# Loading the weights of groups 2 to 4 from SyncE instead of GpSimd in a fused attention and FFN backward kernel

## The chip, the cores and the metric

The kernel runs on one core of one Trainium2 chip. The metric is the device time of one execution in microseconds; the kernel before takes 282.91 us in the median of three runs (282.87 to 283.6). PE is the matrix engine, DVE the vector engine, ACT the scalar engine, POOL is GpSimd and SP is SyncE, which in this kernel does nothing but start DMA transfers.

## The reference, cut to what matters

One decode step with batch 4, model width 512, 32 query heads, 8 key/value heads of width 128 and a window of 1024 cached positions, next to a gated FFN of width 1792. The kernel returns the output and the gradients of all inputs:

```
xn  = layernorm(x)                                   # x: 4 x 1 x 512
q   = (xn @ wq) in 32 heads;  k, v = last 1024 of 4096 cached rows, each head used by 4 queries
o   = softmax(q k^T / sqrt(128)) v
out = x + o @ wo + (gelu(xn @ w_gate) * (xn @ w_up)) @ w_down
return out, d/d(x, k_cache, v_cache, wq, wo, w_gate, w_up, w_down) of <out, grad_out>
```

The gradients of the two caches have the shape of the caches, 4 x 8 x 4096 x 128 each in bf16. Three quarters of them (the rows outside the window) are zero and have to be written all the same. So there is far more to move than to compute: the profile counts 81.01 MB written to memory and 30.68 MB read.

## The kernel before, in words

The FFN part comes first; its three weight matrices lie in a pool that is closed when it is done. Then the attention part runs over four groups t = 0..3 of two key/value heads each (`for t in range(NT)`, line 725). A group needs its keys and values (`kb`, `vb`: two tiles of 1 MiB each, lines 127 to 135) and its slices of the output and query weights (`wo_sb`, `wq_sb`: 1 MiB each, lines 120 to 125). In a group:

- `pre(t)` (line 285) transposes `wo_sb` on PE (L279), multiplies with `wq_sb` (L303), and makes the query rows and the output-gradient rows. It is called for group t+1 in the middle of group t.
- `kv_steps(t, 0, 0)` and `kv_steps(t, 1, 1)` (line 335) transpose the keys and then the values block by block and form the scores and their gradient.
- `softmax`, `softmax_d`, `odq`, `odT` make probabilities and their gradients and the two products with values and keys.
- `fin(t)` (line 537) reads `wo_sb` (L256) and `wq_sb` (L279, `wqT_ps`) a last time; after that the two buffers are free.
- `dvdk` (line 475) makes the cache gradients in eight pieces per tile: a matmul (L484), a copy from PSUM into `stg_dv` or `stg_dk` by ACT or DVE (L97, L98), and after the eighth piece one 1 MiB store. The staging pool has three buffers. `dw(t)` (line 498) makes the weight gradients through `osb_o` and `osb_q`, of 512 KiB a store, from a pool of four.

The pieces of `dvdk` and `dw` stand in a list `bg`, and `tick(n)` takes n of them between the steps of the next group. All engines run their instructions in the order in which the program gives them; there is no scheduler (`manual_schedule`).

The order of transfers matters here. Every store, every zero fill (`zero()`, line 161: a store of 1.5 MiB from a tile of zeros, 32 in all) and every load but two kinds goes out on SP, in program order. SP waits in front of a transfer until its data or its buffer is ready, and everything behind waits too. The framework also gives the transfers started by SP and ACT eight completion semaphores in turn, so one of them is started only when the one eight places before it has landed. The transfers that POOL starts have semaphores of their own and a DMA queue of their own (q0 in the profile; SP's is q1). ACT starts three: `wg_sb` at the beginning and two small outputs at the end.

The line that decides the engine is the default of this argument; group 0 is loaded with `load_w(0, nc.sync)` on line 151, the others by POOL:

```
120    def load_w(t, eng=nc.gpsimd):
121        pool = w_pool[t % 2]
122        wo_t[t] = pool.tile([P, HG, D], BF16, name="wo_sb", tag="wo")
123        eng.dma_start(out=wo_t[t][:], in_=wo_v[t])
124        wq_t[t] = pool.tile([P, ND, CW], BF16, name="wq_sb", tag="wq")
125        eng.dma_start(out=wq_t[t][:], in_=wq_v[t])
```

In memory a row of a `wo` slice is 1 KB long (512 bf16 values) and a row of a `wq` slice 2 KB (1024 values).

Of the kernel before, what the change touches and what calls it, by code (L numbers as in the profile page):

```python
# [18 lines left out]
def kernel(  # L19
# [28 lines left out]
    nc = tc.nc  # L48
# [71 lines left out]
    def load_w(t, eng=nc.gpsimd):  # L120
        pool = w_pool[t % 2]
        wo_t[t] = pool.tile([P, HG, D], BF16, name="wo_sb", tag="wo")
        eng.dma_start(out=wo_t[t][:], in_=wo_v[t])
        wq_t[t] = pool.tile([P, ND, CW], BF16, name="wq_sb", tag="wq")
        eng.dma_start(out=wq_t[t][:], in_=wq_v[t])

    def load_kv(t, k):
        if t >= NT:
            return
        d_, src, nm = ((k_t, A_k_cache, "kb"), (v_t, A_v_cache, "vb"))[k]  # L130
        for g in range(GP):
            tl = kv_pool[t % 2].tile([P, JB, Dh], BF16, name=nm, tag=nm)
            nc.sync.dma_start(out=tl[:].rearrange("p j d -> p (j d)"),
                              in_=src[:, t * GP + g, K0:Sk, :].rearrange("b (m j) d -> m b (j d)", j=JB))
            d_[(t, g)] = tl
# [25 lines left out]
    def zero(n=1):  # L161
        for _ in range(min(n, len(zlist))):
            og, b, g = zlist.popleft()
            store(nc.sync, og[b, g:g + ZR, 0:K0, :].rearrange("g (m j) d -> m g (j d)", m=P // ZR), ztile[:], "zeros")
# [103 lines left out]
    def link(n=1):  # L268
        for _ in range(min(n, len(chain))):
            chain.popleft()()  # L270
# [64 lines left out]
    def kv_steps(t, k, links):  # L335

        zt = (qm_all, dom_all)[k][t % 2]
        blks = (k_t, v_t)[k]
        ps = ps_a.tile([P, WQ], FP32, name="S_ps", tag=("S", "dP")[k])
        st[t][("S", "dP")[k]] = ps[:]  # L340

        def mm(g, q, T_sb):
            c0 = SL - 1 - (g * NQ + q)
            for b in range(B):
                nc.tensor.matmul(ps[b * RB:(b + 1) * RB, :], lhsT=zt[:, b * GP + g, c0:c0 + RB],  # L345
                                 rhs=T_sb[:].rearrange("p (x b) -> p b x", b=B)[:, b, :], start=(g == 0 and q == 0),
                                 stop=(g == GP - 1 and q == NQ - 1), tile_position=(0, b * RB))

        last = None
        for g in range(GP):  # L350
            for q in range(NQ):
                T_ps = transposes([blks[(t, g)][:, q * JQ + j, :] for j in range(JQ)], "T")
                T_sb = tsb.tile([P, JQ * P], BF16, name="T_sb", tag="T")
                evac(T_sb[:], T_ps[:].rearrange("p j x -> p (j x)"), 1024, half=True)
                tick(1)
                link(links)
                if last:
                    mm(*last)
                last = (g, q, T_sb)
                tick(1)  # L360
                link(links)
        mm(*last)
# [57 lines left out]
    def softmax_d(t):  # L420
        s = st[t]

        def a():
            s["Gt"] = attw.tile([P, WQ], FP32, name="Gt", tag="Gt")
            s["gs"] = attw.tile([P, 1], FP32, name="gs", tag="gs")
            nc.vector.tensor_tensor_reduce(out=s["Gt"][:], in0=s["E"][:], in1=s["dP"], scale=1.0, scalar=0.0,
                                           op0=ALU.mult, op1=ALU.add, accum_out=s["gs"][:])

        def b():
            gs_ps = ps_w.tile([P, 1], FP32, name="gs_ps", tag="w")  # L430
            nc.tensor.matmul(gs_ps[:], lhsT=rsum_f, rhs=s["gs"][:], start=True, stop=True)
            cc = attw.tile([P, 1], FP32, name="cc", tag="cc")
            nc.vector.tensor_tensor(out=cc[:], in0=gs_ps[:], in1=s["rr"][:], op=ALU.mult)
            nc.vector.scalar_tensor_tensor(out=s["Gt"][:], in0=s["dP"], scalar=cc[:, 0:1], in1=s["E"][:],
                                           op0=ALU.subtract, op1=ALU.mult)
            s["dS"] = spread(s["Gt"], s["rr"], "dS_s")

        def c():
            s["dST"] = transposed(s["dS"], "dST")

        idle = lambda: None
        chain.extend([a, idle, b, idle, c])
# [24 lines left out]
    def odT(t, k):  # L467
        rows = st[t][("o", "dq")[k]]
        T_ps = transposes([rows[:, g, :] for g in range(GP)], "odT")
        rT = attw.tile([P, GP, B, rep], BF16, name="od_T", tag=f"od_T{k}")  # L470
        for g in range(GP):
            nc.vector.tensor_copy(out=rT[:, g].rearrange("p b r -> p (b r)"), in_=T_ps[:, g, g * 32:g * 32 + B * rep])
        st[t][("oT", "dqT")[k]] = rT
# [243 lines left out]
    with tc.tile_pool(name="kv_b", bufs=GP, reuse_waits="tile") as kv_b, \  # L717
            tc.tile_pool(name="w_b", bufs=1, reuse_waits="tile") as w_b, \
            tc.tile_pool(name="stage", bufs=3, reuse_waits="tile") as stage:
        kv_pool[1], w_pool[1] = kv_b, w_b  # L720
        zero()
        pre(0)
        load_w(1)
        load_kv(1, 0)
        for t in range(NT):
            kv_steps(t, 0, 0)
            if t == 0:
                zero()
                load_kv(1, 1)
                zero()  # L730
            softmax(t)
            kv_steps(t, 1, 1)
            if t == NT - 1:
                zero(4)
            link(len(chain))
            softmax_d(t)
            link()
            odq(t, 0)
            load_kv(t + 2, 1)
            if t + 1 < NT:  # L740
                pre(t + 1)
            link(len(chain))
            odT(t, 0)
            odq(t, 1)
            load_kv(t + 2, 0)
            tick(2)
            odT(t, 1)
            fin(t)
            if t + 2 < NT:
                load_w(t + 2)  # L750
            (k0, k1), (o0, o1, q0, q1) = dvdk(t, 1), dw(t)
            for p in (k0, o0, k1, o1, q0, q1):
                bg.extend(p)
        tick(len(bg))
        zero(len(zlist))

        fin_ps = []
        for o in range(2):
            f_ps = ps_w.tile([B, ND, P], FP32, name="f_ps", tag="w")
            for c in range(ND):  # L760
                nc.tensor.transpose(f_ps[:, c, :], acc[:, o, c, :], ident_f[:])
            fin_ps.append(f_ps)
        acc_o = fin_ps[0][:].rearrange("b c p -> b (c p)")
        acc_d = attw.tile([B, P, ND], FP32, name="acc_d", tag="P_s")
        nc.vector.tensor_copy(out=acc_d[:].rearrange("b p c -> b c p"), in_=fin_ps[1][:])
        acc_d = acc_d[:].rearrange("b p c -> b (p c)")
        out_b = attw.tile([B, D], BF16, name="out_b", tag="pT")
        nc.vector.tensor_tensor(out=out_b[:], in0=acc_o, in1=x4[:], op=ALU.add)
        nc.scalar.dma_start(out=out_0.rearrange("b s d -> (b s) d"), in_=out_b[:])

        s1 = attw.tile([B, 1], FP32, name="s1", tag="m")
        nc.vector.reduce_sum(out=s1[:], in_=acc_d, axis=AX.X)
        pr = attw.tile([B, D], FP32, name="pr", tag="dS_s")
        s2 = attw.tile([B, 1], FP32, name="s2", tag="es")
        nc.vector.tensor_tensor_reduce(out=pr[:], in0=acc_d, in1=xn_f[:], scale=1.0, scalar=0.0,
                                       op0=ALU.mult, op1=ALU.add, accum_out=s2[:])
        nm1 = attw.tile([B, 1], FP32, name="nm1", tag="rr")
        nc.vector.tensor_scalar(out=nm1[:], in0=s1[:], scalar1=-1.0 / D, scalar2=None, op0=ALU.mult)
        nm2 = attw.tile([B, 1], FP32, name="nm2", tag="gs")
        nc.vector.tensor_scalar(out=nm2[:], in0=s2[:], scalar1=-1.0 / D, scalar2=None, op0=ALU.mult)  # L780
        nc.vector.scalar_tensor_tensor(out=pr[:], in0=xn_f[:], scalar=nm2[:, 0:1], in1=acc_d,
                                       op0=ALU.mult, op1=ALU.add)
        nc.vector.tensor_scalar(out=pr[:], in0=pr[:], scalar1=nm1[:, 0:1], scalar2=rstd[:, 0:1],
                                op0=ALU.add, op1=ALU.mult)
        dx_b = attw.tile([B, D], BF16, name="dx_b", tag="E_f")
        nc.vector.tensor_tensor(out=dx_b[:], in0=pr[:], in1=dy4[:], op=ALU.add)
        nc.scalar.dma_start(out=out_1.rearrange("b s d -> (b s) d"), in_=dx_b[:])
# [30 lines left out]
```

## Time and profile before

| what | value |
|---|---|
| median of three runs | 282.91 us |
| profiled execution, its own time | 283.0 us |
| its span from first to last instruction | 281.0 us |
| PE, DVE, ACT, POOL busy | 72%, 58%, 42%, 14% of the span |
| mean granted PE clock | 0.901 |
| bytes moved, mean rate | 112.12 MB, 399 GB/s |
| POOL's loads of the weights | 6 transfers of 1024 KB, 14.7 us (`wo_sb`) and 19.1 us (`wq_sb`) from issue to landing in the median |

The profiled execution takes 2.0 us more than its span, which lie outside the recorded instructions. Busy shares are means over a kernel with different stages. The row "DMA" of the page cuts the span into 40 slices of 7.0 us and shows the busy share of the 16 DMA engines in tenths (9 is 90% or more); "GB/s" is what they moved. A landing time runs from the issue of a transfer to its completion and includes the time that it stands behind others in its queue.

### The profile page before, as it was taken

The numbers are of one execution on the slowest core, as the hardware profiler recorded it, in microseconds if no ns is written. First come the engines' busy times: TensorE is split into PE (matmuls) and PEld (weight loads), VectorE is DVE, ScalarE is ACT, GpSimd is POOL, SyncE is SP. The second block draws the span as 40 slices with busy tenths as digits, with TensorE's granted clock in tenths as the row PEclk, the third lists the DMA queues.
The fourth block names the chain that finished last, engine by engine and source line by source line (L and its number), as shares of the span: only waits on it lengthen the run. The fifth ranks groups of instructions, "written<-read, shape, count | busy, mean of one in ns | idle before, by whom it ended". The sixth has DMA issues, their size and how long they took to land.

```text
span 281.0 us, 6867 instructions
## 1 busy us (share of the span) xinstructions
PE 203.1 (72%) x2972; PEld 138.8 (49%) x2972; DVE 164.1 (58%) x313; ACT 117.8 (42%) x219; POOL 40.1 (14%) x40
## 2 busy tenths in 40 slices
PE   0276699959789889998999299898999599390000
PEld 0265476735456665566775156677556484140000
DVE  7946646645776655577666067767677728386000
ACT  2030386635035418764448056443866038370000
POOL 8600000007002150002250000223000400000000
PEclk9999589986999999999999969999999979977555
DMA  7999999999999999999999999999999999999990
GB/s 264 393 375 431 431 426 417 425 419 424 369 395 424 422 420 420 426 415 422 419 417 411 412 424 423 431 383 398 385 368 415 387 432 410 425 429 422 398 422 30
DMA packets 19565, 112.12 MB, mean 399 GB/s; under 512 B 1664, under 2 KB 4496, under 8 KB 11088
## 3 DMA queue, kind: packets, MB, share of 16 engines
q1 hardware_dynamic: 17744, 103.56, 89.6%
q0 software_dynamic: 1632, 6.29, 5.6%
q10 hardware_dynamic: 160, 1.84, 1.9%
q8 instruction: 23, 0.38, 0.5%
q14 instruction: 6, 0.05, 0.0%
HBM read 30.68 MB, written 81.01 MB: 397 GB/s over the span
## 4 chain that ended last, share of the span: by engine, by line
PE 47%; DMA 22%; DVE 16%; ACT 4%; issue 2%; SPq 0%; DVEq 0%; ACTq 0%
DMA out_dram<-stg_dv 13%; PE T_ps L279 8%; PE kv_ps L484 7%; DMA wd_sb<-in_B_w_down_dram 6%; PE S_ps L345 5%; PE od_ps L450 5%; DMA out_dram<-osb_g 4%; DVE T_sb L98 3%; DVE dS_s L367 2%; PE wdT_ps L279 2%; PE dwq_ps L520 2%; PE acc_ps L256 2%; PE dwd_ps L660 2%; DVE P_s L367 2%; PE wgT_ps L279 2%
## 5 line engine op out<-in xcount | busy, mean ns | idle before, releaser
L98 DVE COPY T_sb<-T_ps 128x1024 bf16<-128x1024 bf16 x64 | 44.1, 688 | 26.7 <-PE T_ps L279 26.5
L97 ACT CAST stg_dk<-kv_ps 128x512 bf16<-128x512 f32 x52 | 29.2, 588 | 31.2 <-PE kv_ps L484 12.4
L97 ACT CAST stg_dv<-kv_ps 128x512 bf16<-128x512 f32 x51 | 28.1, 588 | 24.9 <-PE kv_ps L484 24.3
L484 PE MATMUL kv_ps<-qmr,dS_s 128*128 128x512 bf16 x64 | 23.9, 414 | 11.3 <-ACT stg_dk L97 10.6
L463 POOL TENSOR_TENSOR o_s<-od_r,msk_r 128x512 bf16<-128x512 bf16 x8 | 9.1, 1157 | 110.2 <-DVE od_r L455 80.9
L484 PE MATMUL kv_ps<-domr,P_s 128*128 128x512 bf16 x64 | 21.3, 382 | 0.0
L279 PE MATMUL T_ps<-ident,vb 128*128 128x128 bf16 x256 | 20.3, 225 | 0.4 <-DVE T_sb L98 0.4
L279 PE MATMUL T_ps<-ident,kb 128*128 128x128 bf16 x256 | 20.4, 225 | 0.0
L279 PEld LDWEIGHTS <-kb 128*128 128x128 bf16 x256 | 17.5, 101 | 4.5 <-issue 1.3
L279 PEld LDWEIGHTS <-vb 128*128 128x128 bf16 x256 | 17.2, 101 | 5.0 <-issue 3.2
L97 ACT CAST osb_q<-dwq_ps 128x512 bf16<-128x512 f32 x25 | 14.6, 587 | 8.3 <-PE dwq_ps L520 7.4
L329 POOL TENSOR_TENSOR domr<-r,msk 128x1024 bf16<-128x1024 bf16 x4 | 7.6, 1892 | 71.2 <-DVE r L326 65.1
L97 ACT CAST osb_g<-dwg_ps 128x512 bf16<-128x512 f32 (+1 forms) x25 | 12.3, 544 | 12.3 <-PE dwg_ps L673 6.3
L97 ACT CAST osb_o<-dwo_ps 128x512 bf16<-128x512 f32 x24 | 13.9, 586 | 4.5 <-PE dwo_ps L505 2.9
L98 DVE CAST stg_dk<-kv_ps 128x512 bf16<-128x512 f32 x12 | 8.0, 688 | 12.0 <-DMA out_dram<-stg_dv 11.2
L98 DVE COPY wgT<-wgT_ps 128x1024 bf16<-128x1024 bf16 x14 | 9.6, 686 | 6.8 <-PE wgT_ps L279 6.8
L345 PE MATMUL S_ps<-T_sb,qm 128*32 128x256 bf16 x128 | 12.7, 387 | 0.6 <-DVE T_sb L98 0.5
L345 PE MATMUL S_ps<-T_sb,dom 128*32 128x256 bf16 x128 | 12.7, 388 | 0.1
L505 PE MATMUL dwo_ps<-dyr,o_s 128*128 128x512 bf16 x32 | 12.4, 413 | 0.3 <-ACT stg_dk L97 0.2
L98 DVE COPY woT<-woT_ps 128x1024 bf16<-128x1024 bf16 x16 | 11.0, 686 | 2.7 <-PE woT_ps L279 2.3
L484 PEld LDWEIGHTS <-dS_s 128*128 128x128 bf16 x64 | 6.2, 101 | 12.2 <-issue 11.1
L520 PE MATMUL dwq_ps<-od_r,xnm 128*128 128x256 bf16 x64 | 11.6, 274 | 0.3 <-ACT osb_q L97 0.2
(188 smaller groups left out, 385.0 us busy)
## 6 DMA issues: line engine op xcount, KB each, us to landing
out_dram<-ztile SPq DMA_DIRECT2D x32, 1536.0 KB, 18.1
kb<-in_A_k_cache_dram SPq DMA_DIRECT2D x8, 1024.0 KB, 17.4
vb<-in_A_v_cache_dram SPq DMA_DIRECT2D x8, 1024.0 KB, 20.7
out_dram<-stg_dv SPq DMA_DIRECT2D x8, 1024.0 KB, 13.0
out_dram<-stg_dk SPq DMA_DIRECT2D x8, 1024.0 KB, 20.8
out_dram<-osb_o SPq DMA_DIRECT2D x8, 512.0 KB, 17.4
out_dram<-osb_q SPq DMA_DIRECT2D x8, 512.0 KB, 13.8
out_dram<-osb_g SPq DMA_DIRECT2D x8, 448.0 KB, 14.3
```

The costliest lines, as they stand in the source:

```text
L97: return nc.scalar.copy(out=out, in_=in_)
L98: return nc.vector.tensor_copy(out=out, in_=in_)
L256: nc.tensor.matmul(ps[:, c, :], lhsT=lf(c), rhs=rhs, start=(k == 0), stop=(k == len(terms) - 1))
L279: nc.tensor.transpose(ps[:, i, :], a, ident[:])
L329: nc.gpsimd.tensor_tensor(out=mr[:].rearrange("p g q d -> p (g q) d"), in0=r4[:, k, :].unsqueeze(1).broadcast_to([P, SL, Dh]), in1=msk[:]. ...
L345: nc.tensor.matmul(ps[b * RB:(b + 1) * RB, :], lhsT=zt[:, b * GP + g, c0:c0 + RB], rhs=T_sb[:].rearrange("p (x b) -> p b x", b=B)[:, b, :] ...
L367: nc.vector.scalar_tensor_tensor(out=out[:], in0=src[:].unsqueeze(2).broadcast_to([P, WQ, B]), scalar=rr[:, 0:1], in1=mskb[:].unsqueeze(1) ...
L450: nc.tensor.matmul(od_ps[g * 32:g * 32 + B * rep, k, g, :], lhsT=cols[:, jj, g * NQ + q, :], rhs=blks[(t, g)][:, j, :], start=(j == 0), st ...
L463: nc.gpsimd.tensor_tensor(out=o_s[:, g], in0=rows[:, g].unsqueeze(1).broadcast_to([P, rep, Dh]), in1=msk_r[:].unsqueeze(2).broadcast_to([P ...
L484: nc.tensor.matmul(mps[:].rearrange("p q d -> p (q d)"), lhsT=src[:, j * P:(j + 1) * P], rhs=mr[:, g].rearrange("p q d -> p (q d)"), start ...
L505: nc.tensor.matmul(mps[:], lhsT=o_s[:, g].rearrange("p r d -> p (r d)")[:, i:rep * Dh:rep], rhs=dyr[:], start=True, stop=True)
L520: nc.tensor.matmul(mps[:, i].rearrange("p g d -> p (g d)"), lhsT=xnm[:, i2 * 2 + i, c * P:(c + 1) * P], rhs=dq_r[:].rearrange("p g d -> p ...
```

## The change

The weights of groups 1, 2 and 3 are started by SP, at the same places of the program; the shapes, buffers and every computing instruction stay.

```diff
@@ -720,7 +720,7 @@
         kv_pool[1], w_pool[1] = kv_b, w_b
         zero()
         pre(0)
-        load_w(1)
+        load_w(1, nc.sync)
         load_kv(1, 0)
         for t in range(NT):
             kv_steps(t, 0, 0)
@@ -747,7 +747,7 @@
             odT(t, 1)
             fin(t)
             if t + 2 < NT:
-                load_w(t + 2)
+                load_w(t + 2, nc.sync)
             (k0, k1), (o0, o1, q0, q1) = dvdk(t, 1), dw(t)
             for p in (k0, o0, k1, o1, q0, q1):
                 bg.extend(p)
```

In the built program POOL loses six transfers and SP gains six. On SP the pair of group 1 stands ahead of the keys `kb` of group 1; the pair of group 2 behind the keys of group 2 and ahead of the first `stg_dk` store of group 0; the pair of group 3 behind the second `stg_dv` store of group 1 and a zero fill, and ahead of the first `stg_dk` store of group 1. The six also take places in the rotation of eight semaphores.

## The prediction

> **What bounds the kernel now.** I read the 40 slices of the page first, then its DMA queues.
>
> ```profile
> DMA  7999999999999999999999999999999999999990
> GB/s 264 393 375 431 431 426 417 425 419 424 369 395 424 422 420 420 426 415 422 419 417 411 412 424 423 431 383 398 385 368 415 387 432 410 425 429 422 398 422 30
> ...
> q1 hardware_dynamic: 17744, 103.56, 89.6%
> q0 software_dynamic: 1632, 6.29, 5.6%
> ```
>
> The 16 DMA engines are at 90% or more in 38 of 40 slices. A queue line gives packets, MB and share of 16 engines' span: together 95%, so this kernel is bound by bytes. Full flow is 420 to 430 GB/s, and moving all 112.12 MB at 425 would take 264 us. Time can only come from slices below that. These are the start, slices 11 and 12 (70 to 84 us), and 27 to 32 (183 to 225 us). I measured the stretches directly (columns: stretch, its length, busy us and count of PE, PEld, DVE, ACT, POOL, PE clock, DMA share, GB/s).
>
> ```profile
> 11.00:18.00 7.00, 4.11 (x119) 3.61 (x120) 4.12 (x17) 1.64 (x2) 0.76 (x2) 1.00 1.06 356
> 70.00:80.00 10.00, 8.24 (x105) 5.22 (x103) 7.13 (x15) 1.36 (x4) 0.00 (x0) 1.00 0.99 369
> 155.00:160.00 5.00, 1.05 (x14) 0.59 (x12) 0.00 (x0) 0.00 (x0) 0.00 (x0) 1.00 1.01 419
> 185.00:220.00 35.00, 33.53 (x499) 21.94 (x497) 23.98 (x49) 20.53 (x39) 3.74 (x2) 1.00 0.95 387
> ```
>
> From 185 to 220 the DMA share falls to 0.95 and PE is busy 33.5 of 35 us: stores are made too slowly, (425 - 387) x 35 / 425 = 3.1 us are lost; slice by slice I get 3.4, which I use. From 155 to 160 it is the other way round: the DMA flows at 419 and computing stands still. The chain of waits and the timeline name the reason.
>
> ```profile
> 137.81 23.51 DMA out_dram<-stg_dv
> ...
> 161.41 0.69 DVE L98 CAST stg_dk<-kv_ps 128x512 bf16<-128x512 f32 x1 [6.48 <-DMA out_dram<-stg_dv]
> 161.42 1.07 ACT L97 CAST stg_dk<-kv_ps 128x512 bf16<-128x512 f32 x2 [7.04 <-DMA out_dram<-stg_dv]
> ```
>
> A `stg_dv` store issued at 137.81 lands at 161.32, and DVE and ACT stand 6.5 us for its staging buffer. That stall makes everything later by as much, and the DMA lacks stores from 185 on. At the end the DMA runs full from 225 to 275 with a queue of zeros and stores, so the end moves one for one with work added to the DMA and with idle DMA time.
>
> Last, how POOL's loads share: the queues from 137 to 162, the tail of the queue at 150.95, and the first load of group 0 on SP.
>
> ```profile
> q1 hardware_dynamic: 1488, 8.23, 80.6%
> q0 software_dynamic: 518, 2.04, 20.2%
> ...
> out_dram<-ztile SPq DMA_DIRECT2D x1, 1536.0 KB, 25.6
> ...
> 2.45 8.91 SPq L123 DMA_DIRECT2D wo_sb<-in_A_wo_dram  x1
> 11.40 3.59 SPq L125 DMA_DIRECT2D wq_sb<-in_A_wq_dram  x1
> ```
>
> While that `stg_dv` store waits in q1, 2.04 MB of group 3's weights pass it in q0.
>
> **What the Trainium skill says**, all on the page "DMA: Bandwidth & Descriptors". Section "Issuing engines are not separate DMA queues": transfers run on the same 16 engines whoever issues them, and interleave. The trace agrees: about 420 GB/s with or without q0 traffic from 100 to 165. Section "Queues, rings and completion order": each DMA engine takes turns between queue rows that have work, packet by packet. The trace agrees: q0 gets 20% of the time though it has only one or two transfers against six or eight, and they land after 13 to 22 us while q1's need up to 28. Section "SWDGE vs HWDGE vs iDMA": packets of GpSimd's DMAs are preferably up to 4096 B. The trace shows 1536 data packets of exactly 4096 B in q0, though rows are 1 and 2 KB.
>
> **The change part by part.**
>
> *POOL.* Six issues of 0.76 to 1.06 us go, 5.4 us in all. POOL is idle 86% of the time, and what follows them on POOL (`o_s`) waits 19 us or more for DVE. Worth nothing.
>
> *Packets.* SP's loads of group 0 go out as single rows. In the stretch 11 to 18, q1 has 2347 packets for 2.49 MB, nearly all of 1 KB, in 105.5% of 7 us x 16: 50 ns each; the packet records give 48.7 ns for 1 KB and 85.2 ns for 2 KB. q0's 4 KB take 0.056 x 281.0 x 16 us / 1536 = 164 ns. So one `wo` load costs (1024 x 48.7 - 256 x 164) ns / 16 = +0.5 us and one `wq` load (512 x 85.2 - 256 x 164) / 16 = +0.1 us. Three pairs: +1.8 us of DMA work in a full stretch. It is on the path.
>
> *The slow stretch 70 to 80.* It loses (425 - 369) x 10 / 425 = 1.3 us. It is where group 1's weights in q0 run beside the keys in q1; all packets are longer there (8 KB in 352 ns instead of 310). The other two pairs show no such dip, so I can't say that two queues of reads cause it. The gain is 0 to 1.3 us; I carry both ends.
>
> *SP.* Six more issues at 0.6 us are 3.6 us of SP's time and hidden, if SP does not stick. On group 0 they took 8.9 and 3.6 us, because SP is held while the ring is full of small packets. Behind them wait the keys of group 1 and three `osb_g` stores (pair 1), `stg_dk`, zeros and `osb_o` (pair 2), `stg_dk` again (pair 3). The cover is the queue: transfers there land 17 to 28 us after issue, more than 12.5 us, so DMA has work while SP is stuck, and a store issued later lands no later, as its place in the queue counts. The same holds for the two extra places in the rotation of eight. The keys have time: group 1's are needed at 103.8 and would land by 85.
>
> *Order of landing.* This is what matters. Whatever stands in q1 ahead of a pair no longer shares with it; the pair waits its turn behind. The `stg_dv` store of 161.32 is ahead of pair 3: it gains most of 2.04 MB, (1.84 MB passed before 161.3) / 0.413 = 4.5 us, and loses 1.2 us for the packets of two pairs: 158.0, or 156.7 if the dip goes. The stall of 6.5 us shrinks by 3.3 or 4.6 us, and PE needs `wq_sb` of group 3 not at 179.43 (first use, L303) but at 176.1 or 174.8. The pair now lands right behind the zero fill issued at 150.95, which lands at 176.55 with the old pair already through. So it lands at 176.55 + 1.8 = 178.4, or 177.1: PE waits 2.3 us there, a new wait, and goes on 1.0 or 2.3 us earlier than before. Pair 2: `kb` ahead of it lands at 129.43 now; with the pair taken behind, `wq_sb` lands at 129.4 + 1.2 = 130.6 at worst, against a need at 130.01: 0 to 0.6 us. Pair 1 lands before 80, need 88.3.
>
> *Sum.* Stores from 185 on come 1.0 to 2.3 us earlier, and the DMA is 1.8 or 0.5 us behind: lack of stores shrinks by 2.8 in both cases, from 3.4 to 0.6. Against that +1.8 of packets and 0 to -1.3 of the dip: -1.0 to -2.3 us, middle -1.6. From the profiled 283.0 (281.0 span and 2.0 around it) that is 281.4. The profiled run is 0.1 above the median, which I neglect.
>
> **Rivals.**
>
> *No difference.* Bytes bound the kernel and the order is hidden. For it: 95% DMA share. It needs the recovered idle time and the packet price to cancel, for example if the 3.4 us are unevenly filled engines instead of lacking stores, so only 1.8 returns: 282.2 to 283.6.
>
> *Slower: group 3's weights come too late.* Place: `pre(3)`, where PE works in order and everything waits behind L303. Now the pair has 15 us of slack (landed at 163.9, used at 179.4); after it I leave it none, and from 179.4 on every us of lateness is a us of the end, since stores from 185 on are already short. My margin is 1.0 to 2.3 us. SP reaches the pair only when the `vb` loads eight places before have landed (154.75 and 158.69 now), and then fills the ring with 1536 small packets. Lateness of 3 us gives 286; if the queue also ran dry behind SP, more. Against it: the queue is over 20 us deep there.
>
> *Faster by more.* The dip goes, the clock drop that follows the stall (0.53 from 160 to 165) goes too, and nothing waits in `pre(3)`: 3.4 + 1.3 - 1.8 = 2.9 us, 280.1.
>
> *The change does nothing it says*: excluded, the built order has the six issues on SP.
>
> **How the numbers follow.** A measurement here tells 0.3% (0.85 us), from the runs' spread of 0.73 us. Forecast 0.42 (280.7 to 282.0), more faster 0.12, no difference 0.24, slower 0.22. Faster 0.54, same 0.24, slower 0.22. The forecast's and both neighbours' bounds give 279.8 at the low end; 285.0 takes in most of the slower case.
>
> **What would show it.** q0 gone, and q1 with 3 x (1024 + 512) = 4608 more data packets; `wo_sb` and `wq_sb` landing 20 us or more after issue for pairs 2 and 3. The stall on `stg_dk` near 155 at 1.5 to 3.5 us. A wait of PE on DMA at L303 near 177. 185 to 220 above 400 GB/s. Wrong it would be if the DMA share falls in the stretches where SP issues the pairs (SP stuck, queue dry), if PE gets `wq_sb` of group 3 after 180, or if 70 to 80 stays at 369 and the stall does not shrink.

## The result: 0.25% slower, and the profile after

The changed kernel takes 284.26 us in the median, the kernel before 283.36 us beside it on the same chip: ratio 1.0025, interval 1.0015 to 1.0035. Run again with other experiments it gave 1.0034 (1.0023 to 1.0045). So the change costs 0.7 to 1.0 us, at the edge of what the prediction called no difference, where its 281.4 stands for a gain. Groups count from 0 here, so groups 1 to 3 are the second to the fourth of the title. The profiled execution takes 283.91 us with a span of 282.2 us; before it was 283.0 and 281.0.

The slices and the queue of the changed kernel (one digit or number for each 7.05 us; packets, MB and share of 16 engines):

```profile
DMA  7999999999999999999999999999999999999980
GB/s 273 386 376 431 433 421 420 417 423 414 331 419 427 415 421 426 424 328 427 426 410 425 406 414 383 422 415 429 424 404 414 403 433 416 428 426 419 405 359 21
...
q1 hardware_dynamic: 22448, 109.85, 95.7%
```

q0 is gone, and q1 has 4704 packets more: the 4608 that were predicted and 96 completion writes, 16 for each of six transfers. The numbers 383, 398, 385, 368 of before (slices 27 to 30) are now 415, 429, 424, 404. Slice 18, which was 415, is 328. The stretches of the changed kernel, with the columns of the prediction's table (the last three are PE clock, DMA share, GB/s):

```profile
70.00:80.00 10.00, 7.85 (x98) 5.06 (x97) 7.30 (x15) 0.95 (x4) 0.00 (x0) 1.00 1.03 360
120.00:130.00 10.00, 8.60 (x148) 6.08 (x145) 6.72 (x11) 4.63 (x8) 0.67 (x1) 1.00 1.03 361
155.00:160.00 5.00, 4.93 (x56) 2.82 (x55) 2.79 (x5) 3.59 (x7) 0.00 (x0) 1.00 1.01 409
165.00:175.00 10.00, 8.43 (x145) 5.90 (x141) 6.78 (x13) 4.32 (x8) 0.31 (x1) 1.00 1.01 382
185.00:220.00 35.00, 33.68 (x503) 21.98 (x501) 23.69 (x48) 20.19 (x39) 3.75 (x2) 1.00 1.00 413
```

And two of these stretches in the kernel before, which the prediction did not show:

```profile
120.00:130.00 10.00, 9.30 (x155) 6.49 (x154) 6.69 (x13) 5.28 (x9) 0.00 (x0) 1.00 1.02 423
...
165.00:175.00 10.00, 9.42 (x101) 5.91 (x99) 7.50 (x15) 5.97 (x13) 0.00 (x0) 0.89 1.01 426
```

What was predicted inside did happen. The lack of stores from 185 to 220 has shrunk from 3.1 to (425 - 413) x 35 / 425 = 1.0 us, and from 155 to 160 PE works 4.93 of 5 us, where it had 1.05. The timeline of the changed kernel (start, duration, engine, line; in brackets the idle time before it and what ended that) has the steps:

```profile
130.92 0.35 PE L303 MATMUL doq_ps<-xnT,wq_sb 128*128 128x4 bf16 x8 [1.61 <-DMA wq_sb<-in_A_wq_dram]
...
154.73 13.66 SPq L125 DMA_DIRECT2D wq_sb<-in_A_wq_dram  x1
...
157.66 0.59 ACT L97 CAST stg_dk<-kv_ps 128x512 bf16<-128x512 f32 x1 [0.60 <-DMA out_dram<-stg_dv]
...
178.16 0.37 PE L303 MATMUL doq_ps<-xnT,wq_sb 128*128 128x4 bf16 x8 [2.02 <-DMA wq_sb<-in_A_wq_dram]
```

The stall for the `stg_dv` store is 0.6 us long in place of 7.0; PE waits 1.6 us for group 2's `wq_sb` and 2.0 us for group 3's. And the chain that ended last has the new waits, with the transfers' start and length:

```profile
107.41 23.47 DMA wq_sb<-in_A_wq_dram
...
154.73 23.39 DMA wq_sb<-in_A_wq_dram
```

**Where the gain went.** I counted bytes in the packet records of both profiles and took, for a time T of the kernel before, by how much later the changed kernel had moved as many:

```
T (us)            70    120    130    160    180    200    215    240    260    275
after, later by +0.13  +0.42  +1.89  +1.69  +2.68  +1.74  +0.46  +0.02  -0.11  +0.45
```

By 180 the pairs have cost 2.7 us. By 240 the stores that come in time have given all of it back. At 240 and 260 us the two kernels have moved the same bytes, and still the changed one ends 1.1 us later. What lies between is in the tails. The kernel before:

```profile
255.00:270.00 15.00, 0.00 (x0) 0.00 (x0) 2.78 (x8) 0.00 (x0) 0.00 (x0) 0.53 1.03 421
270.00:273.00 3.00, 0.00 (x0) 0.00 (x0) 0.00 (x0) 0.00 (x0) 0.00 (x0) 0.50 0.96 404
275.00:279.00 4.00, 0.00 (x0) 0.00 (x0) 0.00 (x0) 0.00 (x0) 0.00 (x0) 0.50 0.06 25
279.50:281.00 1.50, 0.00 (x0) 0.00 (x0) 0.00 (x0) 0.00 (x0) 0.00 (x0) 0.50 0.00 0
```

The kernel after:

```profile
255.00:270.00 15.00, 0.00 (x0) 0.00 (x0) 4.48 (x10) 0.00 (x0) 0.00 (x0) 0.62 1.02 421
...
275.00:279.00 4.00, 0.00 (x0) 0.00 (x0) 0.00 (x0) 0.00 (x0) 0.00 (x0) 0.50 0.06 28
279.50:281.00 1.50, 0.00 (x0) 0.00 (x0) 0.00 (x0) 0.00 (x0) 0.00 (x0) 0.50 0.04 16
```

A share of 0.06 is one engine of sixteen, and 25 to 28 GB/s is one packet of 12,288 bytes every 460 ns. Fifteen engines have sent their last packet by 275.2 us before and 275.5 after. One goes on alone and sets the end: its last packet ends at 279.58 before and at 280.71 after, and in both the span ends 1.5 us behind it.

It is late long before. A transfer has landed when all sixteen engines have completed their parts. From its eighth completion to its landing the kernel before takes 0.7 us near 17, 2.0 near 45, 2.6 to 4.6 near 105, up to 8.5 near 155, 5 to 7 from 180 to 210 and 5.5 to 6.1 from 240 on; the kernel after 1.5 to 2.5 near 75, 3.0 near 120, 4.3 to 5.0 near 160 and 7.5 from 240 to 260. The trace has no engine numbers, so that it is the same engine from the beginning is not shown. In the kernel before, the fifteenth completion is at most 1.4 us ahead of the last until 100 us, and often 0.2; from 150 on it is about 2 to 5 us ahead.

The `stg_dk` store that the prediction followed lands at 179.40 before and 180.67 after, 1.27 us later. For the landings, thus for the late engine, this difference stays, 1.1 us at the last fill. The eighth completions of the same transfers go from 2.6 us later to 0.4 earlier in that time.

So the theory to be tested, **A**: the end is the end of one late DMA engine, which in the second half always has work waiting. Work that the change adds to this engine is paid; time in which the other engines lack stores is not. The rival, **B**, is the prediction's own sum: the end follows the total flow, and something else (the dips near 125 and 170, or the new waits of PE) took the gain.

### The profile page after: what moved, and what is told of

It reads as the page before. It is cut to its first block, busy times and chain, and to the rows that moved or that the text cites. A ratio compares the mean times of both kernels' runs of the same rounds, so it can differ in the third digit from the quotient of the medians.

```text
span 282.2 us, 6862 instructions
## 1 busy us (share of the span) xinstructions
PE 207.1 (73%) x2972; PEld 141.7 (50%) x2972; DVE 163.8 (58%) x313; ACT 118.2 (42%) x219; POOL 35.0 (12%) x34
## 4 chain that ended last, share of the span: by engine, by line
PE 40%; DMA 34%; DVE 11%; ACT 5%; issue 1%; SPq 0%; ACTq 0%; DVEq 0%
DMA wq_sb<-in_A_wq_dram 17%; PE kv_ps L484 8%; PE T_ps L279 6%; DMA wd_sb<-in_B_w_down_dram 6%; DMA out_dram<-stg_dv 5%; PE od_ps L450 5%; PE S_ps L345 4%; DMA out_dram<-osb_g 4%; DMA out_dram<-osb_d 3%; PE acc_ps L256 3%; DVE wqT L98 2%; PE woT_ps L279 2%; PE wdT_ps L279 2%; PE wqT_ps L279 2%; DVE dS_s L367 2%; PE pT_ps L279 2%
## 5 line engine op out<-in xcount | busy, mean ns | idle before, releaser
L484 PE MATMUL kv_ps<-qmr,dS_s 128*128 128x512 bf16 x64 | 22.8, 396 | 6.7 <-ACT stg_dk L97 6.0
L484 PE MATMUL kv_ps<-domr,P_s 128*128 128x512 bf16 x64 | 23.0, 409 | 0.0
L279 PE MATMUL T_ps<-ident,vb 128*128 128x128 bf16 x256 | 19.4, 219 | 0.0
L279 PEld LDWEIGHTS <-vb 128*128 128x128 bf16 x256 | 16.4, 98 | 4.1 <-issue 1.8
L484 PEld LDWEIGHTS <-dS_s 128*128 128x128 bf16 x64 | 6.0, 98 | 13.7 <-issue 12.6
L505 PE MATMUL dwo_ps<-dyr,o_s 128*128 128x512 bf16 x32 | 12.6, 420 | 0.3 <-ACT stg_dk L97 0.2
L279 PE MATMUL woT_ps<-ident,wo_sb 128*128 128x128 bf16 x128 | 11.5, 242 | 1.5 <-DMA wo_sb<-in_A_wo_dram 1.4
```

The source lines that it names most:

```text
L279: nc.tensor.transpose(ps[:, i, :], a, ident[:])
L484: nc.tensor.matmul(mps[:].rearrange("p q d -> p (q d)"), lhsT=src[:, j * P:(j + 1) * P], rhs=mr[:, g].rearrange("p q d -> p (q d)"), start ...
L505: nc.tensor.matmul(mps[:], lhsT=o_s[:, g].rearrange("p r d -> p (r d)")[:, i:rep * Dh:rep], rhs=dyr[:], start=True, stop=True)
```

## The experiments

### More lack of stores: a delay of PE where B says that it counts

```diff
+            if t + 2 == NT:
+                spin = ps_w.tile([P, D], FP32, name="spin_ps", tag="w")
+                for _ in range(14):            # 40 in the second kernel
+                    nc.tensor.matmul(spin[:], lhsT=sel[:], rhs=xn_b[:], start=True, stop=True)
             if t + 1 < NT:
```

> The kernel before, with 14 extra matmuls on PE ahead of pre(3), about 3 us of delay for all later computing. Theory A (the end is set by one DMA engine that runs some 6 us behind the other fifteen and never lacks work, so lost or won computing time does not count): 0 to +0.5 us, the DMA share from 185 to 220 falls, the last packets end where they did. Theory B (the end is set by the flow of all 16 engines, so idle time from 185 on counts one for one, as predicted): +2.5 to +3.5 us.

The kernel before, with 14 matmuls that nobody reads ahead of `pre(3)`: ratio 1.0008, interval 0.9997 to 1.0020. They keep PE for 3.2 us (374 ns each, overlapping). Its profile:

```profile
179.58 3.19 PE L743 MATMUL spin_ps<-xn_b,sel 4*128 4x512 bf16 x14
...
185.00:220.00 35.00, 33.52 (x480) 22.29 (x478) 24.92 (x48) 19.63 (x38) 3.74 (x2) 0.97 0.89 364
```

The lack of stores grows: 364 GB/s, (425 - 364) x 35 / 425 = 5.0 us lost in place of 3.1. By the count of bytes the bulk of the engines is 1.4 us late at 160, ahead of the delay, and 3.7 us late at 260. The medians differ by 0.3 us. The landings show it more directly: in this execution they are 0.8 us later than before already at the store of 179.40, ahead of the delay, and 0.9 at the last fill, while the eighth completions go from 1.3 to 3.8 us later. A holds, B falls, which wants 2 us and more. How much is free, the longer delay tells:

> As e1, with 40 extra matmuls of 374 ns[...], 9 to 12 us of delay. In e1 a delay of 3.7 us cost 0.3 us and left the lagging engine 2.9 us behind the others. Theory A: the delay is free until that lag is used up, then counts one for one: 9 to 12 minus about 5, so +4 to +7 us, and the lag at the end is gone. Theory B: the whole delay, +9 to +12 us.

With 40 such matmuls, 1.0316 (1.0272 to 1.0360). The delay, and the tail of this kernel:

```profile
178.09 13.22 PE L743 MATMUL spin_ps<-xn_b,sel 4*128 4x512 bf16 x40
```

```profile
276.00:287.00 11.00, 0.00 (x0) 0.00 (x0) 0.00 (x0) 0.00 (x0) 0.00 (x0) 0.50 1.01 414
287.50:289.00 1.50, 0.00 (x0) 0.00 (x0) 0.00 (x0) 0.00 (x0) 0.00 (x0) 0.50 0.00 0
```

Now the engines end together, at full share to 287; the stretch with one engine is gone. The bulk is 12.6 us late at 260 (0.4 at 180, ahead of the delay), the last packet 8.3 us. So some 4 us of such a delay were free, and the rest is paid; 4.4 us is also the distance between the last two engines at the end of the kernel before. The time alone would not decide here: the medians differ by 8.3 us, by the ratio it is 8.9, above A's 4 to 7 and just under B's 9 to 12, because the delay came out longer than planned: from 184 to 192 the granted clock was 0.50, and a matmul took up to 629 ns. What decides is that the bulk is 12.6 us late and the last packet 8.3. What the prediction meant to win was inside the free part.

### Giving the late engine more work

If the end hangs on one engine, it must move when the last zero fill gives that engine more work. The first try put the last fill of the kernel before (two halves of 768 KB) on twelve engines, in 8 KB packets:

```diff
-        zero(len(zlist))
+        zero(len(zlist) - 1)
+        while zlist:
+            og, b, g = zlist.popleft()
+            for i in range(ZR):
+                store(nc.sync, og[b, g + i, 0:K0, :].rearrange("(m j r) d -> m j (r d)", m=12, r=4096 // Dh),
+                      ztile[0:12, 0:4096].unsqueeze(1).broadcast_to([12, K0 * Dh // 12 // 4096, 4096]), "zeros")
```

> The kernel before with its last zero fill written from 12 partitions in place of 64, in two stores, so that it runs on 12 of the 16 DMA engines. Theory A: the lagging engine is spared 8 packets of 12 KB, 3.7 us, if it is one of the four left out, and the twelve get 1.2 us more: 2.5 to 3.7 us faster; 0 to 1.5 us slower if it is one of the twelve. Theory B: 12 engines carry the last 1.5 MB, about +1 us.

> The changed kernel with the same last zero fill on 12 engines. Theory A: as much faster against the changed kernel as the previous one against the kernel before, and the gap of 0.9 us between the two shrinks to 0 to 0.5 us if the lagging engine no longer ends last, since the other engines stand level at 260 us in both profiles. Theory B: about +1 us against the changed kernel.

Measured 1.0405 (1.0381 to 1.0428) on the kernel before and 1.0349 (1.0316 to 1.0382) on the one after: far more than either theory says, and no test of them. The tail of the first:

```profile
276.00:286.00 10.00, 0.00 (x0) 0.00 (x0) 0.00 (x0) 0.00 (x0) 0.00 (x0) 0.50 0.72 79
```

Twelve engines (0.72 of sixteen) move 79 GB/s together, and an 8 KB packet takes 1253 ns in the median, where it takes 309 elsewhere. All of them read partitions 0 to 11. The Trainium skill, page "SBUF — State Buffer", section "Door 1: The DMA port swizzle", says that four neighbouring partitions share one DMA port; so twelve readers had three ports, four to each: 4 x 309 = 1236. The measurement agrees with the page. The same fill from 24 partitions, every fifth:

```diff
+                store(nc.sync, og[b, g + i, 0:K0, :].rearrange("(m j r) d -> m j (r d)", m=24, r=4096 // Dh),
+                      ztile[0:120:5, 0:4096].unsqueeze(1).broadcast_to([24, K0 * Dh // 24 // 4096, 4096]), "zeros")
```

> The kernel before with its last zero fill on 12 of the 16 DMA engines as in e3, but read from every fifth partition, 24 in all, in place of twelve neighbours (whose 8 KB packets took 1.2 us instead of 0.31). Theory A: 2.5 to 3.7 us faster if the lagging engine is one of the four left out; 0.5 to 1.5 us slower if it is one of the twelve. Theory B: about +1 us.

> The changed kernel with the same last zero fill. Theory A: the same gain as e5 against its own base; the gap of 0.9 us between the two kernels shrinks if the lagging engine no longer ends last. Theory B: about +1 us against the changed kernel.

Now 309 ns for most packets, and 1.0064 (1.0041 to 1.0087) and 1.0107 (1.0089 to 1.0124) of the kernel before. The first kernel has become slower by 1.8 us, the changed one by 2.1 to 2.3, both by more than A (0.5 to 1.5) or B (about 1) allowed, and the gap between the two has not shrunk. The packets say more than the time: near 281 us a single engine is at work with 8 KB packets. So the late engine was among the twelve and got a larger part. With eight engines, from every sixteenth partition:

```diff
+                store(nc.sync, og[b, g + i, 0:K0, :].rearrange("(m j r) d -> m j (r d)", m=8, r=4096 // Dh),
+                      ztile[0:128:16, 0:4096].unsqueeze(1).broadcast_to([8, K0 * Dh // 8 // 4096, 4096]), "zeros")
```

> The kernel before with its last zero fill on 8 DMA engines, read from every 16th partition. Theory A: 1.5 to 2 us faster if the lagging engine is one of the eight left out (the eight end at 274.1 + 3.7 = 277.8 instead of 279.6); 3 to 4 us slower if it is one of the eight used. Theory B: about +3.7 us.

1.0344 (1.0325 to 1.0362), with 638 ns a packet in the median, again not the price that was expected. By the same section partitions 0, 16, 32 and so on to 112 lie on four ports, two readers each: 2 x 309 = 618. The time says nothing on A, but the packets do: from 273 to 276 us seven packets of 8 KB run beside one of 12 KB that belongs to an earlier fill. So the late engine is one of the eight that got this fill. A last kernel uses this. It moves only half a fill (768 KB) with six engines, from partitions on six ports. The trace has no engine numbers; the Trainium skill, page "DMA: Bandwidth & Descriptors", section "Why a DMA increments its semaphore by 16 and not by 1", says that a transfer of SP on k engines uses the lowest k, so the six would be among the eight:

```diff
+        store(nc.sync, og[b, g, 0:K0, :].rearrange("(m j) d -> m (j d)", m=P), ztile[:, 0:K0 * Dh // P], "zeros")
+        store(nc.sync, og[b, g + 1, 0:K0, :].rearrange("(m j r) d -> m j (r d)", m=6, r=4096 // Dh),
+              ztile[0:24:4, 0:4096].unsqueeze(1).broadcast_to([6, K0 * Dh // 6 // 4096, 4096]), "zeros")
```

> The kernel before, its very last half zero fill (768 KB) moved by six DMA engines in place of sixteen, in 8 KB packets of 309 ns from partitions 0, 4, .. 20. The runs with eight and with twelve engines in the last fill showed one packet of 12 KB running beside seven and beside eleven packets of 8 KB, so the late engine is one of the lowest eight. If it isn't one of the lowest six, it is spared 48 KB (four packets of 460 ns, 1.84 us): its last packet ends at 277.7 in place of 279.58; the six start near 272.2 and take 16 packets x 309 ns = 4.9 us, to 277.2; the whole is 1.5 to 2 us faster than before, near 281.4, 0.993 to 0.995. If it is one of the six, it has 16 packets in place of four of 12 KB, 4.9 us for 1.84: last packet near 282.7, 1.010 to 1.012. If the end doesn't hang on the late engine (the reading of the aggregate flow), ten engines idle for the last 3 us of 5, and the whole is 1 to 3 us slower.

1.0105 (1.0071 to 1.0139), or 3.0 us more. This fits the second case, where the late engine is one of the six, and the slow end of B's 1 to 3 us as well, so the time does not decide. The packets do. From 275 to 276 us five packets of 8 KB run beside one of 12 KB. From 279.5 on a single engine works through its 8 KB packets, each 309 ns, until 282.99, where 282.7 was computed for it, and the span ends 1.4 us behind it, as before. So the end follows this one engine when its work is raised by a computed amount. The version that spares it (the last fill on engines without it) was not tried.

### The price of packets, among kernels that load everything with SP

Here the weights of groups 1 to 3 come in rows of 8 KB from the same memory, so each holds other values than the program means and the output is not the reference's.

```diff
         wo_t[t] = pool.tile([P, HG, D], BF16, name="wo_sb", tag="wo")
-        eng.dma_start(out=wo_t[t][:], in_=wo_v[t])
+        if t:
+            eng.dma_start(out=wo_t[t][:].rearrange("p h n -> p (h n)"),
+                          in_=A_wo.rearrange("(t p h) n -> t p (h n)", p=P, h=HG)[t])
...
-        eng.dma_start(out=wq_t[t][:], in_=wq_v[t])
+        if t:
+            eng.dma_start(out=wq_t[t][:].rearrange("p c j -> p (c j)"), in_=A_wq.rearrange("(t p) j -> t p j", p=P)[t])
```

> The changed kernel, but the loads of groups 1 to 3 take rows of 8 KB that lie together in memory, so that SP's packets are as large as those of the keys; the weights stand in the wrong places, so this kernel does not compute the reference, the work and the order stay. Theory A: six loads at 2.50 us instead of 2.62 us of every engine's time, 0.3 to 1.0 us under the kernel before, and about 1.5 us under the changed kernel. Theory B: the same packet gain and the recovered idle time of 2.3 us, 2.5 to 3.5 us under the kernel before. If the place in SP's queue is what costs, not the packet size: as slow as the changed kernel, +0.9 us.

> The changed kernel with wq_sb of groups 1 to 3 taken from 8 KB rows (wrong places of the weights, so it does not compute the reference), wo_sb in 1 KB rows as in the change. Price by packet: 3 x (2.73 - 2.50) = 0.7 us under the changed kernel, about +0.2 against the kernel before. If the two small-packet loads in a row cost more together (the ring full of them): 1 us or more under the changed kernel.

> The changed kernel with wo_sb of groups 1 to 3 taken from 8 KB rows (wrong places of the weights, so it does not compute the reference), wq_sb in 2 KB rows as in the change. Price by packet: 3 x (3.12 - 2.50) = 1.9 us under the changed kernel, about -0.9 against the kernel before. If packet size does not set the price: within 0.4 us of the changed kernel.

| from SP | ratio to before (interval) | last packet |
|---|---|---|
| `wo` 1 KB, `wq` 2 KB (the change) | 1.0025 (1.0015 to 1.0035), again 1.0034 | 280.71, again 280.66 |
| `wo` 1 KB, `wq` 8 KB | 1.0021 (1.0008 to 1.0034) | 279.90 |
| `wo` 8 KB, `wq` 2 KB | 0.9979 (0.9967 to 0.9990) | 279.20 |
| `wo` 8 KB, `wq` 8 KB | 0.9959 (0.9939 to 0.9978) | 278.94 |

From the last row, `wo` in 1 KB packets costs 0.62% = 1.75 us where the durations say 3 x (1024 x 48.7 - 128 x 309) / 16 ns = 1.9 us. `wq` in 2 KB packets costs 0.20% = 0.57 us where they say 0.8; the intervals of these two rows overlap, so this part is not clear of noise. Part of the cost of `wo` is longer packets of the load behind it, as the next section shows. Together they cost 1.9 to 2.1 us. The order of the four is as computed. The last packets are of one execution each, and executions of the same code differ there: just ahead of the delays above, the landings were 0.8 us later than before in one kernel and 0.2 earlier in the other. With 8 KB rows and everything from SP the kernel beats before by 1.2 us, a little over A's 0.3 to 1.0 and far from B's 2.5 to 3.5. So SP as the issuer is not what costs; it costs together with the short rows.

### Each part of the change alone

```diff
-    def load_w(t, eng=nc.gpsimd):
+    def load_w(t, eng=nc.gpsimd, eng_q=None):
...
-        eng.dma_start(out=wq_t[t][:], in_=wq_v[t])
+        (eng_q or eng).dma_start(out=wq_t[t][:], in_=wq_v[t])
...
-                load_w(t + 2)
+                load_w(t + 2, nc.sync, nc.gpsimd)      # wo alone; (nc.gpsimd, nc.sync) for wq alone
```

> Only the wo_sb loads of groups 1 to 3 on SP (rows and packets of 1 KB), wq_sb stays with POOL. Theory A, price by packet: 3 x 0.5 = 1.5 us more work on every DMA engine; the whole change was priced at 1.8 and cost 0.9, so +0.7 to +1.5 us against the kernel before. Theory B (computing and the flow of all engines): -0.5 to -2 us, since the stall at 155 us shrinks.

> The kernel with only the output weights of groups 1 to 3 on SyncE, run again. It had measured 0.9994 of the kernel before, where the price by packet size alone says +1.5 us. If that holds, 0.998 to 1.001 again, its bytes on the majority of engines ahead of before by about 1 us and the last packet near 279.7 us; if the first result was chance, 1.003 to 1.005, the last packet near 280.5 us or later.

> Only the wq_sb loads of groups 1 to 3 on SP (rows and packets of 2 KB), wo_sb stays with POOL. Theory A: 3 x 0.1 us, 0 to +0.4 us against the kernel before. Theory B: -0.5 to -2 us.

> The changed kernel itself again, beside the three others: +0.9 us against the kernel before.

`wo` alone on SP: 0.9994 (0.9984 to 1.0004), and again 0.9995 (0.9982 to 1.0009). A clear miss of the packet price, twice. `wq` alone: 1.0009 (0.9994 to 1.0024), as small as computed. The changed kernel again: 1.0034. So the parts cost about 0.1 us by their medians and the whole 0.7 to 1.0. The tail of `wo` alone, second run:

```profile
255.00:270.00 15.00, 0.00 (x0) 0.00 (x0) 3.16 (x8) 0.00 (x0) 0.00 (x0) 0.57 1.02 421
270.00:273.00 3.00, 0.00 (x0) 0.00 (x0) 0.00 (x0) 0.00 (x0) 0.00 (x0) 0.50 0.84 356
275.00:279.00 4.00, 0.00 (x0) 0.00 (x0) 0.00 (x0) 0.00 (x0) 0.00 (x0) 0.50 0.06 28
```

The bulk is done a us earlier than before (0.84 where before has 0.96 from 270 to 273; 1.26 us ahead at 260 by the count of bytes), and the last packet ends at 279.69, 0.1 later. This is A once more: fifteen engines gain over a us and the time doesn't change.

The packet records show where the parts do not add up. With `wq` alone on SP, its 2 KB packets of groups 2 and 3 take 85.5 and 84.3 ns in the mean. In the changed kernel, right behind `wo` in 1 KB packets, they take 115.0 and 93.6 (109.9 and 101.6 when run again). That is (29.5 + 9.3) x 512 / 16 ns = 1.2 us more of each engine's time in the mean, 1.3 in the second run. `wq` in 8 KB rows behind `wo` in 1 KB is drawn out too, by 0.3 us (120 to 132) and 0.65 us (165 to 180). With `wo` alone, where a store follows on SP, the 8 KB packets of these stretches stay within 0.1 us of before. So most of what the whole change costs goes with a load right behind a load of 1 KB packets in SP's queue. Why these packets get longer, and whether the late engine pays just this mean, was not shown: with `wq` alone the landings are 0.9 us later at the store of 179.40 without longer packets.

Nor is it settled why the late engine pays nothing for 3072 small packets in `wo` alone. In the changed kernel SP is held for 14.06 and 13.66 us in the `wq` issues of groups 2 and 3. When it comes free, four of its transfers have not landed, where before there were eight and seven. But with `wo` alone SP is held on the store behind (8.6 and 14.7 us), and the second time only three have not landed there. So this alone is not the reason.

### Delays early in the kernel

If only the late engine counts, a delay in which that engine too runs out of work must cost its full length. Three kernels give POOL more of the early loads:

```diff
-    load_w(0, nc.sync)
...
+    load_w(0)               # by POOL near 9 us, behind its first memsets; in the third kernel near 12 us
```

> The kernel before with wd_sb and the weights of group 0 loaded by POOL as well, so that their packets are 4 KB in place of 1, 1 and 2 KB; the other direction of the change. Theory A: (1792 x 48.7 - 448 x 164) ns / 16 = 0.86 us for wd_sb, 0.5 for wo_sb, 0.1 for wq_sb: 0.7 to 1.5 us faster than the kernel before. Theory B: the same bytes, and the start of computing later by what POOL takes to begin: 0 to +2 us.

> The kernel before with the weights of group 0 loaded by POOL behind its first fills, about 9 us in, in place of SP: 4 KB packets in place of 1 and 2 KB, used from 53 us on. Price by packet: 0.6 us faster than the kernel before. If wd_sb, which would share with them, lands late enough to hold up the start (17.8 us now): 0 to +2 us, as in e11, where it landed at 24.5.

> The kernel before with the fourth pair of weights, group 0's, loaded by GpSimd as well, but issued behind GpSimd's own start-up work, near 12 us, so that the down-projection's weights (landing at 17.8 us before, held up until 24.1 us when GpSimd issued the pair near 9 us) are through or nearly so. Packet price: the pair costs +0.5 and +0.1 us more in SyncE's 1 and 2 KB packets, so 0.6 us less here: 282.6 us if the down-projection's weights still land by 18 to 19 us. If GpSimd's 4 KB packets hold them up again by more than 2 us, PE starts later and the whole is 0 to 2 us slower than before (283.3 to 285).

The first (`wd_sb` by POOL too) gives 1.0191 (1.0161 to 1.0220), the second 1.0191 (1.0171 to 1.0212), the third 1.0034 (1.0015 to 1.0053). All three were meant to win by the packet price and lost, the first two by more than the 0 to 2 us that their other case allowed. In the second `wd_sb`, which SP loads in 1 KB packets, lands near 24.1 us in place of 17.8:

```profile
24.13 1.14 PE L279 MATMUL wdT_ps<-ident,wd_sb 128*128 128x128 bf16 x9 [6.00 <-DMA wd_sb<-in_B_w_down_dram]
```

and 20 us later all engines run short (before had 416 GB/s and a share of 1.00 here):

```profile
40.00:50.00 10.00, 9.33 (x108) 6.66 (x109) 4.31 (x7) 7.70 (x15) 0.00 (x0) 0.70 0.57 230
```

The bulk is 6.1 us late at 260, and the last packet 6.1 us later: nothing is free here. In the first it is 5.1 and 5.4 us. The profiled execution of the third is 2.7 us above its own median, so only its sign is used.

## Why the prediction was wrong, by its own steps

**What bounds the kernel: here it failed.** The sentence was that "the end moves one for one with work added to the DMA and with idle DMA time". The first half held where work was put on the late engine (in the run on six engines 3.1 us were computed, and its last packet came 3.4 us later). The second is true only of idle time of the late engine, which the prediction took for one of sixteen equal ones. 3.1 us of lacking stores shrank to 1.0 (foreseen: 3.4 to 0.6), and that was worth nothing, because the end had some 4 us of room for such a delay (12.6 us of it cost 8.3). The view that shows it was on the page: the last number of the GB/s row is 30 for the 7 us from 274, and a share of 0.06 from 275 to 279 is one engine. I read that row for slices below the full flow and passed over the last one as a mere end.

**POOL.** Nothing here speaks against its worth of 0. No run took only its issues away.

**Packets: right sign, wrong parts.** The count was exact. Of +1.8 us came +1.1 on the last packet and 0.7 to 1.0 in the medians, but that this is near the forecast is in part luck: `wo` alone, priced at 1.5, costs nothing in two runs. The 48.7 ns is a mean of the first 20 us in which some packets are long (the median is 46); in the three pairs of the changed kernel 1 KB packets take 49.4, 47.7 and 46.9 ns in the mean, and those of 2 KB 96, 115 and 94, where 85.2 was put in. The prediction priced each load by itself and had no term for a load that stands behind one of small packets. Why `wo` alone costs nothing stays open.

**The slow stretch.** 360 GB/s from 70 to 80, so no gain. The lower end of 0 to 1.3 was right: one queue has the dip too.

**SP.** Held 5.3 us in the first pair and 14 us in the others, against 12.5 foreseen. "The cover is the queue" held for the late engine so far as its difference in landing is constant afterwards; it did not hold for the total flow, which fell from 423 to 361 and from 426 to 382 GB/s, (62 + 44) x 10 / 425 = 2.5 us in two stretches with a full DMA share: the packets got longer, 2 KB ones up to 225 ns in the mean from 122 to 124 us. The prediction had no term for that.

**Order of landing: right in the main.** `stg_dv` lands near 157.6 (foreseen 158.0 or 156.7), PE goes on in `pre(3)` at 178.16 (178.4 or 177.1), group 2's `wq_sb` lands at 130.88, 0.3 us over the worst case foreseen. The stall shrank more than foreseen, by over 6 us, since ACT came to it 2.7 us later than before.

**Sum.** -2.8 for the stores becomes 0, the dip 0, and +1.8 becomes the +0.9 that was measured. The last is no second forecast: put in from the runs, it leads back to the profiled 283.91.

**Rivals.** "No difference" came nearest; its 282.2 to 283.6 ends 0.3 us short of the profile, and it deserved more than 0.24. Its example, unevenly filled engines instead of lacking stores, hits only half: the stores did lack, but the late engine was 5 us and more behind in these stretches and had work left. "Group 3's weights come too late" did not occur: they came at 178.12, and PE at the same place at 183.16, after the first delay, still costs only 0.2 us. "Faster by more" fell with the first step.

## What to carry to other kernels

Before time is counted as won because the DMA engines idle less, look at the last 5 to 10 us: if the DMA share there is 1/16 for several us, one engine sets the end, and only what makes that engine's own work shorter, or starves it, moves the time. A delay that costs nothing is the cheapest test of it. And where a load is moved between SP and POOL, count its packets at durations measured in that part of the kernel, and run each part alone: here the parts did not add up.

## What was not expected of the hardware

- One of the sixteen DMA engines ends last by over 4 us, in this kernel and in the changed one. Measured from the eighth completion it is 6.0 us behind at 240 us before and 7.5 after, and no further from there on. The Trainium skill, page "DMA: Bandwidth & Descriptors", section "Latency and other measured facts", says that engines 7 and 15 are usually slower and guesses at the rings of GpSimd's transfers. Here it is late without any data transfer by GpSimd too. If a transfer on k engines uses the lowest k, as the section cited above says, the run on six engines puts it among engines 0 to 5, so not 7 or 15. One engine ends last in this way on several chips (5.6 us behind the fifteenth in `wo` alone on one, 6.1 us with 8 KB rows on another). Why it is late was not found.
- Readers of one SBUF port divide it: most 8 KB packets take 309 ns alone, 638 with two and 1253 with four engines on a port, with the ports as the skill's page has them.
- A queue of 4 KB packets beside one of 1 KB packets takes more than half: with GpSimd's loads beside `wd_sb`, q0 had 61% of the engines' time from 12 to 18 us, and 1.8 MB in 1 KB packets landed at 24.1 in place of 17.8 us.
- SP is held up to 15.1 us by one issue when a load of 1024 small packets is the last ahead of it, whatever it issues next.
- Packets of a load right behind a load of 1 KB packets on SP's queue take longer: 2 KB in 115 and 94 ns in the mean, against 84 to 86 without it.
